# Decode attention with an MLP beside it: wq and wo read like keys inside the loop, and w1 added up by POOL

## The chip, the cores and the metric

The kernel runs on one core of a Trainium2 chip, all in float32. The metric is the time of one execution on the device in microseconds (us), as the median of several runs. Besides, the hardware profiler recorded one execution.

## The reference, cut to what matters

```python
xn = layernorm(x)                               # x: 512 numbers
q = (xn @ wq).reshape(32, 128)                  # wq: 512 x 4096; 32 heads of queries
k, v = repeat each of the 8 heads 4 times       # caches: 8 x 65536 x 128
p = softmax(q k^T / sqrt(128))
a = (p v).reshape(4096) @ wo                    # wo: 4096 x 512
b = relu(xn @ w1) @ w2                          # w1: 512 x 1792, w2: 1792 x 512
return x + a + b
```

There is one token. K and V are 268 MB each, wq and wo 8.4 MB each, w1 and w2 3.7 MB each: 561 MB that are read once.

## The kernel before, in words

K and V are taken as 32 chunks of 16384 positions, four chunks to each of the 8 key heads. One chunk is 8.4 MB. There is one buffer for K (`kt`), one for V (`vt`) and one for w1 and later w2 (`wt`), so a chunk's transfer can start only when the chunk before it in the same buffer has been used up.

All large transfers are issued by SP, one after the other, in the order of lines 135 to 156: wq in two halves into `vt`, w1 into `wt`, the first K into `kt`; then in a loop V after semaphore `vfree`, the next K after `kfree`; at the end wo in four parts into `kt`, and w2 in four parts into `wt`. SP waits at each of these semaphores, and what stands behind a wait in its list waits too. ACT issues two small transfers of x (L190, L192); in the first, each of the 128 partitions gets four numbers.

The head (before the loops). ACT, PE, DVE and POOL make the layer norm; POOL ends it with xn (L178 to L182). Element `p*4+a` of a vector lies on partition p, column a. DVE then multiplies the first two of wq's four blocks by xn and adds them (L338, L339), PE adds up the partitions and the other two blocks (L235) into one row, and DVE transposes that row into `qbig`. The same is done with w1 (L245), giving h, and `hT` after the ReLU (L356).

The loop over chunks on PE (L251): scores (L259), 8 rounds of four matmuls of 512 columns. The four go to four strips of 32 rows, c = 0 to 3, and run side by side; each pair of rounds fills two PSUM banks, which DVE transposes into `tr` (L365) and gives back by `free`. After the last pair DVE signals `kfree` (L364). DVE takes the maximum (L369 to L376), with the help of two small PE steps (L266, L268); ACT computes the exponentials (L212); PE multiplies them with V (L275, "PV"); DVE signals `vfree` (L378) and copies the result (L379), PE folds it (L282, L285), and DVE keeps the running sums (L381 to L384). In a float32 matmul PE records two weight loads and two matmuls, so 32 matmuls are 64 records.

The tail. When the last head's output `oT` is ready (L387), PE multiplies the last columns of oT with wo (L299), then hT with the first ten rows of blocks of w2 (L307), all added up in four strips of PSUM, `y4`. DVE adds x and copies y4 (L391); PE adds up the strips (L323) between the last four blocks of w2 (L316), which go to `yacc`. DVE copies (L393), and SP writes the output in four pieces of 512 bytes (L156). Then POOL waits for the output.

```python
take(sp, sem("vfree"))
sp.dma_start(vt, v_row[bass.ds(n, 1)]...).then_inc(sem("v"), 16)
take(sp, sem("kfree"))
sp.dma_start(kt, k[0, bass.ds(n + 1, 1)]...).then_inc(sem("k"), 16)
```

`take` is an instruction that waits for a semaphore and lowers it; it is recorded under line 48, and waits at it appear as "PEq L48" or "DVEq L48".

Of the kernel before, what the change touches and what calls it, by code (L numbers as in the profile page):

```python
# [8 lines left out]
AF = mybir.ActivationFunctionType  # L9
ALU = mybir.AluOpType  # L10
# [13 lines left out]

HKV = 1
# [6 lines left out]
TW = 512  # L32
SUB = TW // 32
CHUNK = 16384
NCH = SK // CHUNK
TPC = CHUNK // (CT * TW)
NB = CHUNK // P
XA = D // P
BANKS = 4
WIDE = 4  # L40
WO_CUTS = [8, 8, 8, 8]
# [4 lines left out]
def take(e, sem, n=1):  # L46

    return e.sem_inc(sem, -n).wait_op(sem, n, "sem-ge")  # L48


@with_exitstack
def attention_and_mlp_kernel(
# [25 lines left out]

    kt = sbuf("kt", P, CHUNK)
# [5 lines left out]
    qbig = sbuf("qbig", P, NQ, 32)  # L85
    hbig = sbuf("hbig", P, FB, 32)
    o_sb = sbuf("o_sb", P, WIDE, DH)
    ysum = sbuf("ysum", P, 512)
    x4 = sbuf("x4", P, 512)
# [11 lines left out]
    qpad = sbuf("qpad", P, 32)  # L101
    hT = sbuf("hT", P, FB)
    oT = sbuf("oT", P, NQ)
    m = sbuf("m", P, GROUP)
# [5 lines left out]
    corr = sbuf("corr", P, GROUP)  # L110
    part_sum = sbuf("part_sum", P, GROUP)
    l_run = sbuf("l_run", P, GROUP)
    o_run = sbuf("o_run", P, GROUP)
    ysb = sbuf("ysb", P, P)
# [3 lines left out]
    hrow = banks[:, 1024:1536]  # L118
    acc = banks[:, 2048:2560]
    pma = banks[:, 2560:3072]  # L120
    pmb = banks[:, 3072:3584]
    y4 = banks[:, 3584:]
    yacc = banks[:, :P]
# [6 lines left out]
    half = CHUNK // 2  # L130
    wo_at = [sum(WO_CUTS[:i]) for i in range(len(WO_CUTS) + 1)]
    w2_at = [sum(W2_CUTS[:i]) for i in range(len(W2_CUTS) + 1)]


    for i in range(2):
        cut = slice(i * half, (i + 1) * half)
        sp.dma_start(vt[:, cut], wq_row[:, cut]).then_inc(sem(f"wq{i}"), 16)
    sp.dma_start(wt, w1_row).then_inc(sem("w1"), 16)
    sp.dma_start(kt, k[0, 0]).then_inc(sem("k"), 16)
# [8 lines left out]
    for i in range(len(WO_CUTS)):  # L148
        cut = slice(wo_at[i] * D, wo_at[i + 1] * D)
        sp.dma_start(kt[:, cut], wo_row[:, cut]).then_inc(sem(f"wo{i}"), 16)  # L150
    sp.wait_ge(sem("wfree"), 1)
# [4 lines left out]
    sp.dma_start(out.rearrange("(c n) -> c n", c=CT), ysb[0:P:32, :]).then_inc(sem("out"), 16)  # L156


    def after(ins):

        ins.then_inc(sem("pool"), 1)
        take(pool, sem("pool"))

    pool.memset(x4, 0.0).then_inc(sem("x4z"), 1)
# [3 lines left out]
    after(pool.memset(ident, 0.0))  # L168
    after(pool.affine_select(
# [4 lines left out]
    after(pool.tensor_add(sel, places[0], places[1]))  # L174
    after(pool.tensor_add(sel, sel, places[2]))
    pool.tensor_add(sel, sel, places[3])
    pool.wait_ge(sem("ln"), 4)
    after(pool.tensor_mul(st[:, 6:7], st[:, 5:6], st[:, 5:6]))  # L178
    after(pool.tensor_mul(st[:, 6:7], st[:, 6:7], st[:, 3:4]))
    after(pool.tensor_scalar(st[:, 6:7], st[:, 6:7], -0.5, 1.5, op0=ALU.mult, op1=ALU.add))  # L180
    after(pool.tensor_mul(st[:, 7:8], st[:, 5:6], st[:, 6:7]))
    pool.tensor_scalar_mul(xn, xc, st[:, 7:8]).then_inc(sem("xn"), 1)  # L182
    pool.memset(qpad, 0.0)
    pool.memset(nb_run, 3.0e38)
    pool.memset(l_run, 0.0)
    pool.memset(o_run, 0.0).then_inc(sem("sel"), 1)
# [4 lines left out]
    act.wait_ge(sem("x4z"), 1)  # L191
    act.dma_start(x4[0:1, :], x.rearrange("(o n) -> o n", o=1)).then_inc(sem("x4"), 16)  # L192
# [15 lines left out]
    with act.Fori(0, NCH):  # L208
        take(act, sem("bias"))
        act.activation(corr, diff, AF.Exp)  # L210
# [8 lines left out]
    pe.wait_ge(sem("means"), 1)  # L219
    pe.wait_ge(sem("zero"), 1)  # L220
    pe.wait_ge(sem("ln"), 1)
    pe.matmul(pma[:, 0:1], minus, st[:, 0:1], start=True, stop=True).then_inc(sem("mean"), 1)
    pe.wait_ge(sem("ln"), 2)
    pe.matmul(pmb[:, 0:1], plus, st[:, 2:3], start=True, stop=True).then_inc(sem("mean"), 1)
    pe.wait_ge(sem("xn"), 1)
    for a in range(1, XA):
        if a == 1:
            pe.wait_ge(sem("sum"), 1)
        if a == 2:
            pe.wait_ge(sem("wq1"), 16)  # L230
        src, col = (tr2, ones[:, :1]) if a == 1 else (vt[:, a * NQ * DH : (a + 1) * NQ * DH], xn[:, a : a + 1])
        for i in range(2):
            heads = src.rearrange("p (i h e) -> p i h e", i=2, e=DH)[:, i]
            for c in range(CT):
                last = pe.matmul(  # L235
                    banks[32 * c : 32 * c + 1, i * 512 : (i + 1) * 512], col,
                    heads[:, :, 32 * c : 32 * c + 32], start=(a == 1), stop=(a == XA - 1),
                )
    last.then_inc(sem("qrow"), 1)
    pe.wait_ge(sem("sum"), 2)  # L240
    for a in range(1, XA):
        src, col = (tr2[:, :DFF_ALL], ones[:, :1]) if a == 1 else (wt[:, a * DFF_ALL : (a + 1) * DFF_ALL], xn[:, a : a + 1])
        blocks = src.rearrange("p (b e) -> p b e", e=P)
        for c in range(CT):
            last = pe.matmul(  # L245
                hrow[32 * c : 32 * c + 1, : FB * 32], col,
                blocks[:, :, 32 * c : 32 * c + 32], start=(a == 1), stop=(a == XA - 1),
            )
    last.then_inc(sem("hrow"), 1)
    pe.wait_ge(sem("sel"), 1)  # L250
    with pe.Fori(0, NCH):  # L251
        take(pe, sem("q"))
        take(pe, sem("k"), 16)
        for s in range(TPC):
            if s % 2 == 0:
                take(pe, sem("free"))
            for c in range(CT):
                lo = (s * CT + c) * TW
                last = pe.matmul(  # L259
                    pair[s // 2 % 2][32 * c : 32 * c + 32, s % 2 * 512 : s % 2 * 512 + 512], qpad,  # L260
                    kt[:, lo : lo + TW], start=True, stop=True,
                )
            if s % 2:
                last.then_inc(sem("score"), 1)
        take(pe, sem("m"))
        pe.transpose(pma[:GROUP, :P], m, ident).then_inc(sem("mT"), 1)  # L266
        take(pe, sem("dg"))
        pe.matmul(pmb[:, :GROUP], ones[:GROUP, :], dg, start=True, stop=True).then_inc(sem("nb"), 1)  # L268
        take(pe, sem("probs"))
        take(pe, sem("v"), 16)  # L270
        n = NB // WIDE
        for i in range(n):
            c = 32 * (i % CT)
            b = i * WIDE
            last = pe.matmul(  # L275
                acc[c : c + WIDE * GROUP, :],
                probs[:, b : b + WIDE, :].rearrange("p b g -> p (b g)"),
                vt[:, b * DH : (b + WIDE) * DH],
                start=(i < CT), stop=(i >= n - CT),
            )  # L280
        last.then_inc(sem("acc"), 1)
        pe.matmul(pma[:, 256 : 256 + GROUP], ones, part_sum, start=True, stop=True)  # L282
        take(pe, sem("o"))
        for b in range(WIDE):
            last = pe.matmul(  # L285
                pma[:, 264 : 264 + GROUP], o_sb[:, b, :], sel[:, b, :],
                start=(b == 0), stop=(b == WIDE - 1),
            )
        last.then_inc(sem("part"), 1)

    for j in range(NQ):
        if j in wo_at:
            pe.wait_ge(sem(f"wo{wo_at.index(j)}"), 16)
        if j == 0:
            pe.wait_ge(sem("oT"), HEADS - 1)
        if j == NQ - GROUP:
            pe.wait_ge(sem("oT"), HEADS)
        c = 32 * (j % CT)
        pe.matmul(  # L299
            y4[c : c + 1, :], oT[:, j : j + 1], kt[:, j * D : (j + 1) * D],  # L300
            start=(j < CT), stop=False,
        )
    for b in range(W2_ROWS):
        if b in w2_at:
            pe.wait_ge(sem(f"w2{w2_at.index(b)}"), 16)
        c = 32 * (b % CT)
        last = pe.matmul(  # L307
            y4[c : c + 1, :], hT[:, b : b + 1], wt[:, b * D : (b + 1) * D],
            start=False, stop=(b >= W2_ROWS - CT),
        )  # L310
    last.then_inc(sem("y4"), 1)
    for b in range(W2_ROWS, FB):
# [7 lines left out]
        if b + 1 == w2_at[-2]:  # L320
            pe.wait_ge(sem("ysum"), 1)
            for c in range(CT):
                pe.matmul(  # L323
                    yacc[32 * c : 32 * c + 1, :], sel[:, 0, :1], ysum[:, c * P : (c + 1) * P],
                    start=False, stop=False,
                )
    last.then_inc(sem("yacc"), 1)


    def then(ins):  # L330

        ins.then_inc(sem("dve"), 1)
        take(dve, sem("dve"))

    def add_first_two(src, n, name):

        dve.wait_ge(sem(name), 16)
        then(dve.tensor_scalar_mul(tr2[:, :n], src[:, :n], xn[:, 0:1]))  # L338
        dve.scalar_tensor_tensor(  # L339
# [83 lines left out]
```

## Time and profile before

| | us |
|---|---|
| median of 3 runs (1305.24 to 1305.49) | 1305.4 |
| the profiled execution | 1305.23 |
| its span, from first to last instruction | 1303.5 |
| PE busy | 685.0 |
| DVE busy | 282.3 |
| ACT busy | 75.4 |
| POOL busy | 3.4 |

In the rows of a timeline the first number is the start in us from the begin of the span, the second the time it took; then engine, line, operation, what it writes and reads, how many records were merged, and in brackets the idle time before it with what ended it. In the windows view the columns are: stretch, its length, busy time (and number of instructions) of PE, PEld, DVE, ACT and POOL, granted clock of PE, share of the 16 DMA engines that is busy, GB/s. DMA rows end with the us from issue to landing. Packets are counted in a window by their start or end, so that in short windows the share can go over 1.

### The profile page before, as it was taken

The page shows a single profiled execution, that of the slowest core. Times are in us where ns is not written, and L with a number is a line of the kernel's source. Part 1 is how long each engine was busy: PE and PEld are TensorE (multiplying, and loading weights), DVE is VectorE, ACT ScalarE, POOL GpSimd, SP SyncE. Part 2 cuts the span into 40 slices and gives each one's busy share as a digit, 9 for nine tenths or more (in the row PEclk, how much of TensorE's full clock was granted, in tenths as well). Part 3 has the DMA queues.
Part 4 walks back from the last instruction along what each step waited for, and adds up shares of the span by engine and source line. Part 5 has one row for each costly group of instructions (what it writes and reads, how often), then busy time and mean ns, then how long its engine had stood idle before and what let it go on. Part 6 is the DMA issues. An engine that isn't in the chain of part 4 may idle for free. (4 is left out here: it accounts for less than half of the span.)

```text
span 1303.5 us, 11851 instructions
## 1 busy us (share of the span) xinstructions
PE 685.0 (53%) x4712; PEld 210.0 (16%) x4712; DVE 282.3 (22%) x524; ACT 75.4 (6%) x299; POOL 3.4 (0%) x22
## 2 busy tenths in 40 slices
PE   1554654554554554564465465465456456456547
PEld 0111111111111111111111111111111111111111
DVE  3301222211222211222221122221122221122220
ACT  1000000000000000000000000000000000000000
POOL 1000000000000000000000000000000000000000
PEclk9767777867776776776677776777676776677678
DMA  9999999999999999999999999999999999999998
GB/s 402 451 419 448 420 448 418 451 417 448 420 438 430 426 442 422 446 422 446 422 446 422 446 418 451 418 448 420 440 428 430 438 422 446 422 446 422 446 415 345
DMA packets 10957, 561.04 MB, mean 430 GB/s; under 512 B 1349, under 2 KB 1353, under 8 KB 1610
## 3 DMA queue, kind: packets, MB, share of 16 engines
q1 hardware_dynamic: 10808, 561.00, 99.5%
q8 instruction: 2, 0.03, 0.0%
q10 hardware_dynamic: 146, 0.00, 0.0%
q14 instruction: 1, 0.01, 0.0%
HBM read 560.99 MB, written 0.00 MB: 430 GB/s over the span
## 5 line engine op out<-in xcount | busy, mean ns | idle before, releaser
L259 PE MATMUL banks<-kt,qpad 128*32 128x512 f32 x2048 | 297.7, 743 | 263.2 <-PEq L48 263.2
L275 PE MATMUL banks<-vt,probs 128*16 128x512 f32 x2048 | 293.5, 737 | 173.9 <-PEq L48 173.9
L365 DVE STREAM_TRANSPOSE tr<-banks 128x1024 f32<-128x1024 f32 x128 | 160.0, 1250 | 415.2 <-DVEq L48 415.2
L259 PEld LDWEIGHTS banks<-kt,qpad 128*32 128x32 f32 x2048 | 79.3, 132 | 456.8 <-issue 456.7
L275 PEld LDWEIGHTS banks<-vt,probs 128*16 128x16 f32 x2048 | 69.4, 113 | 371.3 <-issue 371.3
L379 DVE COPY o_sb<-banks 128x512 f32<-128x512 f32 x32 | 22.1, 691 | 446.0 <-DVEq L48 446.0
L210 ACT ACTIVATE corr<-diff 128x4 f32<-128x4 f32 x32 | 6.6, 205 | 1179.7 <-ACTq L48 1179.7
L212 ACT ACTIVATE probs<-tr,nb_new 128x128 f32<-128x128 f32 x128 | 63.8, 507 | 0.0
L266 PE MATMUL banks<-ident,m 128*4 128x128 f32 x32 | 10.1, 317 | 88.3 <-PEq L48 88.3
L285 PE MATMUL banks<-sel,o_sb 128*128 128x4 f32 x256 | 32.8, 252 | 25.4 <-PEq L48 25.4
L285 PEld LDWEIGHTS banks<-sel,o_sb 128*128 128x128 f32 x256 | 31.0, 191 | 27.2 <-issue 27.2
L369 DVE TENSOR_REDUCE m<-tr 128x4 f32<-128x512 f32 x32 | 32.2, 1006 | 2.9
L268 PE MATMUL banks<-dg,ones 4*128 4x4 f32 x64 | 14.3, 291 | 30.1 <-PEq L48 30.1
L212 ACT ACTIVATION_READ_ACCUMULATOR probs<-tr,nb_new 128x1 f32 x128 | 23.9, 187 | 0.0
L266 PEld LDWEIGHTS banks<-ident,m 128*4 128x4 f32 x32 | 2.6, 81 | 116.4 <-issue 116.4
L268 PEld LDWEIGHTS banks<-dg,ones 4*128 4x128 f32 x64 | 12.4, 240 | 37.7 <-issue 37.7
L381 DVE TENSOR_TENSOR l_run<-l_run,corr 128x4 f32<-128x4 f32 x32 | 5.2, 163 | 42.3 <-DVEq L48 42.3
L282 PEld LDWEIGHTS banks<-part_sum,ones 128*128 128x128 f32 x64 | 9.5, 188 | 27.2 <-issue 27.2
L371 DVE TENSOR_REDUCE mg<-banks 4x1 f32<-4x128 f32 x32 | 8.9, 279 | 19.6 <-DVEq L48 19.6
L282 PE MATMUL banks<-part_sum,ones 128*128 128x4 f32 x64 | 12.3, 263 | 0.0
L374 DVE TENSOR_TENSOR nb_new<-banks,nb_run 128x4 f32<-128x4 f32 x32 | 5.2, 162 | 23.8 <-DVEq L48 23.8
L235 PE MATMUL banks<-tr,ones 128*1 128x512 f32 x16 | 3.6, 1048 | 11.3 <-DVE tr L339 11.3
(74 smaller groups left out, 92.8 us busy)
## 6 DMA issues: line engine op xcount, KB each, us to landing
vt<-wq SPq DMA_DIRECT2D x2, 4096.0 KB, 16.8
kt<-wo SPq DMA_DIRECT2D x4, 2048.0 KB, 21.1
wt<-w SPq DMA_DIRECT2D x1, 3584.0 KB, 29.5
wt<-w SPq DMA_DIRECT2D x1, 1536.0 KB, 30.9
wt<-w SPq DMA_DIRECT2D x1, 1024.0 KB, 32.9
wt<-w SPq DMA_DIRECT2D x2, 512.0 KB, 34.1
kt<-k SPq DMA_DIRECT2D x32, 28.6
vt<-v SPq DMA_DIRECT2D x32, 29.2
```

The costliest lines, as they stand in the source:

```text
L210: act.activation(corr, diff, AF.Exp)
L212: last = act.activation(probs[:, :, g], tr[:, :, g], AF.Exp, bias=nb_new[:, g : g + 1], scale=scale, accum_out=part_sum[:, g : g + 1],)
L259: last = pe.matmul(pair[s // 2 % 2][32 * c : 32 * c + 32, s % 2 * 512 : s % 2 * 512 + 512], qpad, kt[:, lo : lo + TW], start=True, stop=True,)
L266: pe.transpose(pma[:GROUP, :P], m, ident).then_inc(sem("mT"), 1)
L268: pe.matmul(pmb[:, :GROUP], ones[:GROUP, :], dg, start=True, stop=True).then_inc(sem("nb"), 1)
L275: last = pe.matmul(acc[c : c + WIDE * GROUP, :], probs[:, b : b + WIDE, :].rearrange("p b g -> p (b g)"), vt[:, b * DH : (b + WIDE) * DH], ...
L282: pe.matmul(pma[:, 256 : 256 + GROUP], ones, part_sum, start=True, stop=True)
L285: last = pe.matmul(pma[:, 264 : 264 + GROUP], o_sb[:, b, :], sel[:, b, :], start=(b == 0), stop=(b == WIDE - 1),)
L365: dve.transpose(tr[:, s * 2 * SUB : (s + 1) * 2 * SUB, :].rearrange("p b i -> p (b i)"), pair[s % 2]).then_inc(sem("free"), 1)
L369: dve.reduce_max(m, tr.rearrange("p b i -> p i b")[:, :GROUP, :], axis=AX.X).then_inc(sem("m"), 1)
L371: then(dve.reduce_max(mg, pma[:GROUP, :P], axis=AX.X))
L379: dve.tensor_copy(o_sb.rearrange("p b d -> p (b d)"), acc).then_inc(sem("o"), 1)
```

## The change

Part by part:

- wq is loaded into `kt` (in three parts, 8192, 4096 and 4096 columns) and scored by PE like a chunk of keys, with xn in the first four columns of the query `qpad`. POOL copies xn there. DVE picks the needed products out of `tr` and adds them up into `qall` with one reduction. SP waits for `kfree` before the first K is issued.
- wo is loaded into `kt` in three parts at the end and scored in the same way with oT as the query; DVE reduces the result to `yT`, spreads it over a diagonal (`yd`), and one matmul of ones adds it into y4.
- The PE loop therefore has 34 turns. Each turn does, if it is not one of the first two, the four matmuls on the added-up w1 (with `kfree`), then the maximum, PV and the folding of the chunk before; and then the scores of the next chunk. In the first two turns the upper part is jumped over.
- POOL multiplies the four blocks of w1 by xn and adds them up in place: four products and three sums of 128x1792. h is read from PSUM only after the loop; hT comes from POOL, and w2 is issued after it.
- Around the loop stands another of two turns, and its body is under an If that is true only in the second turn. In the first turn PE jumps from the start of its code over the loop and comes back.
- K is laid out in memory so that a matmul of strip c reads 16 runs of 32 columns, 128 apart. The transfers have the same shapes as before.
- x goes into y4 as the row `xrow` by a matmul; the output leaves from 128 partitions, four numbers each. `vfree` and `kfree` come from PE; waits are put onto the instructions themselves in many places; running sums l and o are kept in one tile.

```diff
-TW = 512
-SUB = TW // 32
+TPC = 128
+SUB = 1
...
+ROUNDS = 8
+WQ_CUTS = [8192, 4096, 4096]
+WO_CUTS = [16, 8, 8]
...
+    hrow = pmb[:, 64:512]
...
+    def of_own_row(cols, groups):
+
+        return bass.AP(tr.tensor, tr.offset, [list(tr.ap[0]), [32, cols], [32 * cols + 1, groups]])
...
-        sp.dma_start(vt[:, cut], wq_row[:, cut]).then_inc(sem(f"wq{i}"), 16)
+    for i in range(len(WQ_CUTS)):
+        cut = slice(wq_at[i], wq_at[i + 1])
+        sp.dma_start(kt[:, cut], wq_row[:, cut]).then_inc(sem(f"wq{i}" if i else "k"), 16)
     sp.dma_start(wt, w1_row).then_inc(sem("w1"), 16)
+    take(sp, sem("kfree"))
     sp.dma_start(kt, k[0, 0]).then_inc(sem("k"), 16)
...
-    sp.wait_ge(sem("wfree"), 1)
+    sp.wait_ge(sem("hT"), 1)
...
+    sp.dma_start(out.rearrange("(p a) -> p a", p=P), ysb[:, 0, :]).then_inc(sem("out"), 16)
...
+    pool.memset(qpad, 0.0).then_inc(sem("vfree"), 1)
...
+    after(pool.tensor_copy(qpad[:, :XA], xn), "pool", chain[0]).then_inc(sem("q"), 1)
...
+    pool.wait_ge(sem("w1"), 16)
+    for a in range(XA):
+        last = pool.tensor_scalar_mul(w1_of[a], w1_of[a], xn[:, a : a + 1])
...
+    after(pool.tensor_add(w1_of[0], w1_of[0], w1_of[1]), "pool", chain[0])
+    link(pool.tensor_add(w1_of[2], w1_of[2], w1_of[3]))
+    after(pool.tensor_add(w1_of[0], w1_of[0], w1_of[2]), "pool", chain[0]).then_inc(sem("sum"), 1)
...
+    after(pool.tensor_scalar_max(hT, hbig[:, :, 0], 0.0), "hx").then_inc(sem("hT"), 1)
...
+    def tensor_loop():
...
+        with pe.Fori(0, NCH + 2) as t:
+            with pe.If(t > 1):
+                pe.wait_ge(sem("sum"), 1)
+                for c in range(CT):
+                    last = pe.matmul(
+                        hrow[32 * c : 32 * c + 1, :], ones[:, :1], hb[:, :, 32 * c : 32 * c + 32],
+                        start=True, stop=True,
+                    )
+                last.then_inc(sem("kfree"), 1)
...
+                pe.matmul(lo_new[:, 0, :], ones, part_sum, start=True, stop=True).then_inc(sem("vfree"), 1)
...
+            take(pe, sem("q"))
+            take(pe, sem("k"), 16)
+            for s in range(ROUNDS):
+                if s % 2 == 0:
+                    take(pe, sem("free"))
+                for c in range(CT):
+                    last = pe.matmul(
+                        pair[s // 2 % 2][32 * c : 32 * c + 32, s % 2 * 512 : s % 2 * 512 + 512], qpad,
+                        kb[:, s * 16 : s * 16 + 16, c, :], start=True, stop=True,
+                    )
...
+    with pe.Fori(0, 2) as turn:
+        with pe.If(turn > 0):
+            tensor_loop()
+
+    pe.wait_ge(sem("hT"), 1)
+    pe.wait_ge(sem("xrow"), 16)
+    pe.matmul(y4[0:1, :], ones[0:1, 0:1], xrow, start=True, stop=False)
...
+    after(
+        pe.matmul(y4[0:1, :], ones[:, :1], yd.rearrange("p q n -> p (q n)"), start=False, stop=True), "yd"
+    ).then_inc(sem("p2d"), 1)
...
+    def turn_scores(gates=(), free=None):
+
+        for s in range(ROUNDS // 2):
+            if free and s == ROUNDS // 2 - 1:
+                after(dve.nop(), "p2d", s + 1).then_inc(sem(free), 1)
+            ins = after(dve.transpose(tr2[:, s * 1024 : (s + 1) * 1024], pair[s % 2]), "p2d", s + 1)
+            if s < len(gates):
+                ins = after(dve.drain(), gates[s], 16)
+            ins.then_inc(sem("free"), 1)
...
+    turn_scores(["wq1", "wq2"], free="kfree")
+    dve.drain()
+    dve.tensor_reduce(qall, of_own_row(NQ, XA), axis=AX.X, op=ALU.add).then_inc(sem("dve"), 1)
...
+    dve.tensor_copy(qpad, oT).then_inc(sem("q"), 1)
+    dve.transpose(ysum[:, : FB * 32], hrow).then_inc(sem("hx"), 1)
+    turn_scores(["wo1", "wo2"])
+    dve.drain()
+    dve.tensor_reduce(yT, of_own_row(CT, NQ), axis=AX.X, op=ALU.add).then_inc(sem("dve"), 1)
+    after(
+        dve.tensor_mul(
+            yd, ident.unsqueeze(1).to_broadcast([P, CT, P]), yT.unsqueeze(2).to_broadcast([P, CT, P])
+        ), "dve",
+    ).then_inc(sem("yd"), 1)
+    after(dve.tensor_copy(ysum, y4), "p2d", 5).then_inc(sem("ysum"), 1)
```

More of the change, by code (lines that the diff above doesn't have):

```diff
@@ L48, in take, with starts @@
     return e.sem_inc(sem, -n).wait_op(sem, n, "sem-ge")
+def starts(cuts):
+    return [sum(cuts[:i]) for i in range(len(cuts) + 1)]
 @with_exitstack
@@ L129, in attention_and_mlp_kernel @@
     v_row = v[0].rearrange("(n p b) d -> n p (b d)", p=P, b=NB)
[L130 to L137, printed above, removed]
+    wq_at, wo_at, w2_at = starts(WQ_CUTS), starts(WO_CUTS), starts(W2_CUTS)
+    def of_own_row(cols, groups):
[3 more added lines that the diff above has]
+        sp.dma_start(kt[:, cut], wq_row[:, cut]).then_inc(sem(f"wq{i}" if i else "k"), 16)
     sp.dma_start(wt, w1_row).then_inc(sem("w1"), 16)
+    take(sp, sem("kfree"))
     sp.dma_start(kt, k[0, 0]).then_inc(sem("k"), 16)
@@ L155, in attention_and_mlp_kernel, with link @@
     sp.wait_ge(sem("y"), 1)
[L156 to L164, printed above, removed]
+    sp.dma_start(out.rearrange("(p a) -> p a", p=P), ysb[:, 0, :]).then_inc(sem("out"), 16)
+    chain = [0]
+    def link(ins):
+        if chain[0]:
+            after(ins, "pool", chain[0])
+        chain[0] += 1
+        return ins.then_inc(sem("pool"), 1)
     pool.memset(minus, -1.0 / D)
@@ L167, in attention_and_mlp_kernel @@
     pool.memset(eps, EPS).then_inc(sem("means"), 1)
[L168 to L169 removed]
+    link(pool.memset(ident, 0.0))
+    link(pool.affine_select(
         out=ident, in_=ident, compare_op=ALU.not_equal, fill=1.0, base=0,
@@ L181, in attention_and_mlp_kernel @@
[L181 to L186, printed above, removed]
+    link(pool.tensor_add(sel, places[0], places[1]))
+    link(pool.tensor_add(sel, sel, places[2]))
+    link(pool.tensor_add(sel, sel, places[3]))
+    pool.memset(qpad, 0.0).then_inc(sem("vfree"), 1)
+    pool.memset(nb_run, 3.0e38).then_inc(sem("free"), 2)
@@ new lines, in attention_and_mlp_kernel @@
+    w1_of = [wt[:, a * f : (a + 1) * f] for a in range(XA)]
+    pool.wait_ge(sem("w1"), 16)
+    for a in range(XA):
+        last = pool.tensor_scalar_mul(w1_of[a], w1_of[a], xn[:, a : a + 1])
+    last.then_inc(sem("pool"), 1)
+    chain[0] += 1
+    after(pool.tensor_add(w1_of[0], w1_of[0], w1_of[1]), "pool", chain[0])
+    link(pool.tensor_add(w1_of[2], w1_of[2], w1_of[3]))
+    after(pool.tensor_add(w1_of[0], w1_of[0], w1_of[2]), "pool", chain[0]).then_inc(sem("sum"), 1)
+    hbig = ysum[:, : FB * 32].rearrange("p (b i) -> p b i", i=32)
@@ L216, in attention_and_mlp_kernel @@
         last.then_inc(sem("probs"), 1)
[L219 to L302, printed above, removed]
+    kb = kt.rearrange("p (b c e) -> p b c e", c=CT, e=32)
+    hb = wt[:, :f].rearrange("p (b e) -> p b e", e=P)
@@ L323, in attention_and_mlp_kernel @@
                 pe.matmul(
-                    yacc[32 * c : 32 * c + 1, :], sel[:, 0, :1], ysum[:, c * P : (c + 1) * P],
+                    yacc[32 * c : 32 * c + 1, :], ones[:, :1], ysum[:, c * P : (c + 1) * P],
                     start=False, stop=False,
                 )
[L327 to L339, printed above, removed]
-            tr2[:, :n], src[:, n : 2 * n], xn[:, 1:2], tr2[:, :n], op0=ALU.mult, op1=ALU.add
-        ).then_inc(sem("sum"), 1)
+    last.then_inc(sem("p2d"), 1)
```

152 lines of the change are left out of this document (82 added, 70 removed).

## The prediction, made before the changed kernel was run

> **What bounds the kernel now.** I read the page first, for the queues and for the chain that ended last.
>
> ```profile
> q1 hardware_dynamic: 10808, 561.00, 99.5%
> q8 instruction: 2, 0.03, 0.0%
> ...
> DMA wt<-w 3%; SPq L150 0%; SPq L154 0%; PE banks L316 0%; DVE ysb L393 0%
> ```
>
> One queue, SP's, keeps the 16 DMA engines busy for 99.5% of the span, and the chain ends in the last weight transfer. No compute engine sets the pace. How far compute is from setting it shows the timeline of PE, DVE and SP in the first iterations.
>
> ```profile
> 50.99 9.18 PE L259 MATMUL banks<-kt,qpad 128*32 128x512 f32 x64 [6.96 <-PEq L48]
> 60.43 1.25 DVE L365 STREAM_TRANSPOSE tr<-banks 128x1024 f32<-128x1024 f32 x1 [0.62 <-DVEq L48]
> 60.58 0.34 SPq L144 DMA_DIRECT2D kt<-k  x1
> 70.16 9.75 PE L275 MATMUL banks<-vt,probs 128*16 128x512 f32 x64 [5.67 <-PEq L48]
> 91.07 9.61 PE L259 MATMUL banks<-kt,qpad 128*32 128x512 f32 x64 [9.03 <-PEq L48]
> 110.28 8.47 PE L275 MATMUL banks<-vt,probs 128*16 128x512 f32 x64 [4.97 <-PEq L48]
> 129.78 9.04 PE L259 MATMUL banks<-kt,qpad 128*32 128x512 f32 x64 [8.89 <-PEq L48]
> ```
>
> PE starts on a chunk when it has landed. The next K is issued at 60.58 while V lands only near 70.1, so the queue never runs dry: 9.5 us to spare. From 91.07 to 129.78 lie two chunks, 19.35 us each. But from V at 70.16 to K at 91.07 it is 20.91 us, where the same step later takes 129.78 - 110.28 = 19.50. So 1.41 us were lost once. In that stretch lies one of the two packets of q8, 16 KB of instructions; the other lies between 270 and 300 us. The DMA view of the two stretches:
>
> ```profile
> q8 instruction: 1, 0.02, 0.3%
> q8 instruction: 1, 0.02, 0.2%
> ```
>
> My reading: a packet puts one DMA engine behind, and since each transfer is split evenly over the engines, every landing after it waits for that engine. A second packet on another engine then costs nothing more. The end agrees; the view by windows, whose last but one column is the DMA share:
>
> ```profile
> 1297.00:1297.50 0.50, 0.47 (x8) 0.10 (x8) 0.00 (x0) 0.00 (x0) 0.00 (x0) 1.00 0.69 270
> 1297.50:1298.00 0.50, 0.50 (x8) 0.00 (x0) 0.00 (x0) 0.00 (x0) 0.00 (x0) 1.00 0.19 74
> 1298.50:1299.00 0.50, 0.44 (x20) 0.14 (x12) 0.40 (x1) 0.00 (x0) 0.00 (x0) 1.00 0.12 49
> ```
>
> A share of 0.19 is three engines of 16, 0.12 two: they run alone for up to 1.3 us. So the time before is even streaming, about 1.3 us of stragglers, and a head and a tail of some microseconds. Only these can change by much.
>
> **The change part by part.**
>
> *The main loop.* The same bytes land in the same order. K is now laid out so that a matmul reads 16 runs of 32 columns. The old wq code read such runs:
>
> ```profile
> 13.73 0.56 PE L222 MATMUL banks<-st,minus 128*128 128x1 f32 x2 [13.73 <-ACT xc L199]
> 19.90 0.30 POOL L182 TENSOR_SCALAR xn<-xc,st 128x4 f32<-128x4 f32 x1 [0.21 <-POOLq L48]
> 30.74 3.87 PE L235 MATMUL banks<-vt,xn 128*1 128x512 f32 x32
> ```
>
> That is 0.48 us per four records, against 9.18 / 16 = 0.57 for K, so nothing is lost. K's release now comes from PE, after its back edge, the If and one group of four w1 matmuls. With 1 to 2 us for the group by the same rows and some for branches I take 2, allow 4, and 9.5 are to spare: nothing. Were that cover gone, each microsecond would cost one per chunk. V's release moves from DVE to PE at about the same moment, and DVE's fewer small operations are as hidden as before.
>
> *The head.* Before, wq lay in vt, so K's first chunk was queued at once behind w1. Now wq lies in kt, and SP waits for the wq scores before it issues K; the first V and everything else stand behind K in SP's order.
>
> ```profile
> 0.91 0.87 SPq L137 DMA_DIRECT2D vt<-wq  x2
> 1.82 0.45 SPq L138 DMA_DIRECT2D wt<-w  x1
> 2.31 0.67 SPq L139 DMA_DIRECT2D kt<-k  x1
> ```
> ```profile
> wt<-w SPq DMA_DIRECT2D x1, 3584.0 KB, 29.5
> xT<-x ACTq DMA_DIRECT2D x1, 2.0 KB, 12.4
> kt<-k SPq DMA_DIRECT2D x1, 48.4
> ```
> ```profile
> 1.80:2.00 0.20, 0.00 (x0) 0.00 (x0) 0.00 (x0) 0.00 (x0) 0.16 (x2) 1.00 2.39 655
> ```
>
> xn is ready at 20.20; its copy to qpad takes another 0.3; the wq scores are a full key chunk, 9.2 us (I bound them by 8.4 and 10.1, since the half-speed clock that follows an idle stretch ends at varying moments: 9.18, 9.61 and 9.04 above); the release and SP take 0.4 (60.58 against 50.99 + 9.18). The later parts of wq have landed by then. K is issued at 30.1. In an idle queue the first bytes move 0.9 us after the issue (0.91 to 1.8), and I allow the last engine 0.9 more. Before, K's landing was seen at 2.31 + 48.4 = 50.7. Issued at 30.1 it is seen at 30.1 + 0.9 to 1.8 + 19.35 + some 0.4 until a landing is seen: 50.8 to 51.7. So the **gap** is 0.1 to 1.0 us; with the bounds of the scoring, from hidden to 1.9. I take 0.8, near the upper end, because the slowest engine decides.
>
> *The stragglers.* PE has less code outside its loop (the 36 matmuls of wq and w1 and the 32 of wo are gone), and it touches its second page in the first microseconds, while it has nothing to do until 13.73. If the q8 packets are its own, they leave the stretch in which they cost something: an engine 1.4 us behind near 30 us catches up in the gap. At the end 1.3 us can go, at least nothing (if packets come all the same); one of the three may stay. I take -0.8.
>
> *POOL* now adds up w1 in seven operations of 128x1792, from w1's landing at 1.82 + 29.5 = 31.3 on. No row has such an operation on POOL.
>
> ```profile
> L338 DVE TENSOR_SCALAR tr<-wt,xn 128x1792 f32<-128x1792 f32 x1 | 1.1, 1112 | 0.0
> L339 DVE SCALAR_TENSOR_TENSOR tr<-wt,xn,tr 128x1792 f32<-128x1792 f32 x1 | 2.1, 2085 | 0.1
> L175 POOL TENSOR_TENSOR sel<-sel,ident 128x16 f32<-128x16 f32 x1 | 0.2, 220 | 0.2 <-POOLq L48 0.2
> L178 POOL TENSOR_TENSOR st<-st 128x1 f32<-128x1 f32 x1 | 0.2, 193 | 14.6 <-DVE st L346 14.6
> L180 POOL TENSOR_SCALAR st<-st 128x1 f32<-128x1 f32 x1 | 0.2, 190 | 0.2 <-POOLq L48 0.2
> ```
>
> DVE's rows for the size give 4 x 1.11 + 3 x 2.09 = 10.7 us, the lower bound. POOL's TENSOR_TENSOR grows by 27 ns for 15 elements, 1.8 ns each, so 3.4 us an operation and 24 in all. The upper bound is TENSOR_SCALAR, 190 to 299 ns for three elements more: 65 us an operation. I take 24, since that row differs by elements alone. PE needs the sum for K's release, and all of PE's loop stands behind that wait. The next K must be issued by about 68, so the sum is due at 66: 35 us for 24, nothing. [...]
>
> *The tail.* wo was 16 groups of matmuls whose first 24 hid behind its landing; now it is a full scoring.
>
> ```profile
> 1284.89 0.17 DVE L387 TENSOR_TENSOR oT<-o_run,diff 128x4 f32 x1
> 1290.84 1.90 PE L299 MATMUL banks<-kt,oT 128*1 128x512 f32 x16 [0.50 <-DMA kt<-wo]
> 1297.03 1.04 PE L307 MATMUL banks<-wt,hT 128*1 128x512 f32 x8 [0.61 <-DMA wt<-w]
> 1298.21 0.69 DVE L391 TENSOR_TENSOR ysum<-banks,x 128x512 f32<-128x512 f32 x1 [13.16 <-PE banks L307]
> 1298.96 0.40 PE L323 MATMUL banks<-ysum,sel 128*1 128x128 f32 x8
> 1299.48 0.62 PE L316 MATMUL banks<-wt,hT 128*1 128x128 f32 x16
> 1300.16 0.29 DVE L393 COPY ysb<-banks 128x128 f32<-128x128 f32 x1 [1.26 <-PE banks L316]
> 1300.48 0.66 SPq L156 DMA_DIRECT2D y<-ysb  x1
> ```
>
> oT is ready at 1285.06 and qpad by 1285.4; with 9.3 us scoring ends at 1294.7. A group of four strips is 0.86 us (1.90 for two, 1.04 for one: 0.18 is latency). On strip 0 follow the x row, b=0 and b=4, to 1297.3, then w2's second part, to 1298.2, and the new yd matmul, to 1299.1; before, y4 was complete at 1298.07. DVE's copy (0.14 + 0.69), ysum's matmuls (0.46), the last two rows (0.68) and the transpose (0.35) lead to 1301.4, against 1300.48 before: **+0.95**, from +0.75 (scoring of 8.4, w2 sets the start) to +1.65 (10.1). yd hides: DVE's last transpose ends at 1296.3, and a reduction and a product of 512 elements, under 1.4 together by the 0.69 of L391, end before 1298.2; later than that, each microsecond costs one. w2 is now issued after hT, and only the output stands behind that wait: 1285.4, a transpose under 1.25, a short POOL step, so 1287.0, first bytes 1287.9 to 1288.8. wo streams to 1290.8, on early engines to 1289.4: hidden by a little. The output goes out in 128 pieces instead of 4. The nearest row is x, 128 pieces, 12.4 us, but each of an engine's 8 pieces waits there for a wq packet of 32 KB, 1.2 us at 433 GB/s / 16. Without these 9.7 us, 2.7 remain, no more than the 3.0 from 1300.48 to the end of the 1303.5 us span. I take 0 and allow 0.8.
>
> Sum against the profiled execution: 1305.23 + 0.8 - 0.8 + 0.95 = 1306.2. The median of before lies 0.17 above its profiled execution, so **1306.4**.
>
> **The rivals.** About 0.2%, 2.6 us, is what a measurement of this kernel can tell from no change.
>
> (B) The change doesn't do what it says: instruction packets still come while the stream is full. Then 0.8 isn't gained: 1307.2, by the bounds up to 1308.5. For it: the second packet came in mid-loop, where no new code begins. Chance 0.18.
>
> (C) A little faster: scoring of 8.4 hides the gap and all stragglers go, 0 - 1.3 + 0.75: 1304.9. Chance 0.14.
>
> (D) Slower, by pages fetched again. If the If and the back edge drop a page at each pass, two packets come per pass, 66 in all. Each puts one engine 1.4 us behind; spread evenly over 16 that is 5.8 us, and the 0.8 isn't gained: 1313. It decides from about 30 packets on. Against it: 32 back edges before brought two packets. [...] Chance 0.07.
>
> (E) POOL needs more than 35 us: at 7 us an operation the sum ends at 80 and one K is 13 us late: 1319. Chance 0.03.
>
> (F) Head and tail both long: slow clock in both scorings, or PE back from its second page after 13.73. Gap 1.9, stragglers -0.4, tail and output 2.4: 1309.3. Chance 0.10.
>
> **How the numbers follow.** The forecast has 0.48; its own bounds are those of its three terms. The range from 1304.6 to 1309.4 takes in B, C and F and leaves out D, E and some edges. Faster by over 0.2% would be below 1302.8, for which neither head nor tail has room: 0.02, C's edge. Slower: D, E, F and 0.03 of B, 0.23. Within: 0.75.
>
> **What would show it.** In the profile after: PE's first scores near 20.6, for 9 us; the first K issued near 30, and a dip of the DMA share of under a microsecond behind w1; q8 packets, if any, before 30; no step of 20.9 us between chunks; fewer stragglers in the last windows; and 2 us instead of 1.05 between the last landing and the output's issue. A first K issued well after 31, a K released later than V lands, or tens of q8 packets would make the prediction wrong.

## The result, and the profile after

The changed kernel takes **1307.4 us** (median of 22 runs, 1305.7 to 1309.4), the one before 1305.3 (22 runs beside it, 1305.1 to 1306.6). The ratio is 1.0015, with a 95% interval of 1.001 to 1.0021. The change costs 2.1 us: little, but the interval leaves out no change. Its profiled execution took 1308.47 us, with a span of 1306.8, so it lies 1.1 above the median; the times read from it below are to be taken with that reserve.

The page of the changed kernel:

```profile
q1 hardware_dynamic: 10944, 561.00, 99.3%
q8 instruction: 1, 0.02, 0.0%
...
DMA wt<-w 1%; PE banks L315 0%; PE banks L320 0%; DVE ysum L392 0%; DVE ysum L383 0%; PE banks L326 0%; DVE ysb L394 0%; PE banks L333 0%; SPq L167 0%; POOL hT L214 0%; DVE qpad L382 0%; DVEq L358 0%
...
xT<-x ACTq DMA_DIRECT2D x1, 2.0 KB, 13.8
```

SP's queue still fills the DMA engines, now for 99.3% instead of 99.5%; 0.2% of 1306.8 us are 2.6 us. There is one q8 packet where there were two; the DMA view from 4 to 8 us has it:

```profile
q8 instruction: 1, 0.02, 1.4%
```

By its start it comes at 5.3 us. x comes 1.4 us later than before (13.8 for 12.4). The timeline of its head and first chunks:

```profile
14.70 0.20 ACT L227 ACTIVATE xc<-xT 128x4 f32<-128x4 f32 x1 [11.51 <-DMA xT<-x]
...
21.94 9.10 PE L297 MATMUL banks<-kt,qpad 128*32 128x512 f32 x64 [4.46 <-PEq L49]
...
31.23 0.33 SPq L152 DMA_DIRECT2D kt<-k  x1
...
32.88 19.12 POOL L207 TENSOR_SCALAR wt<-wt,xn 128x1792 f32<-128x1792 f32 x4 [11.38 <-DMA wt<-w]
...
33.27 4.43 DVE L359 COPY qpad<-qall 128x4 f32 x1 [0.34 <-DVEq L49]
...
52.09 3.96 POOL L210 TENSOR_TENSOR wt<-wt 128x1792 f32<-128x1792 f32 x1
...
55.33 9.47 PE L297 MATMUL banks<-kt,qpad 128*32 128x512 f32 x64 [24.29 <-PEq L49]
...
64.19 0.11 PEld L261 LDWEIGHTS banks<-wt,ones 128*1 128x1 f32 x4 [0.30 <-POOL wt L212]
...
65.82 0.34 SPq L157 DMA_DIRECT2D kt<-k  x1
...
74.54 8.39 PE L276 MATMUL banks<-vt,probs 128*16 128x512 f32 x64 [5.85 <-PEq L49]
...
94.04 8.89 PE L297 MATMUL banks<-kt,qpad 128*32 128x512 f32 x64 [9.18 <-PEq L49]
```

POOL starts when it has seen w1 land (32.88), and PE's second scoring when it has seen K land (55.33): 22.45 us, where K alone needs 19.35. From there the pace is that of before: 19.50 from V to the next K, and no step of 20.9. K's second chunk is issued at 65.82, over 8 us before V is seen at 74.54. Its tail:

```profile
1286.34 0.16 DVE L379 TENSOR_TENSOR oT<-lo_run,diff 128x4 f32 x1
...
1287.43 5.36 PE L297 MATMUL banks<-kt,qpad 128*32 128x512 f32 x48 [1.92 <-PEq L49]
...
1287.91 1.75 SPq L167 DMA_DIRECT2D wt<-w  x4
...
1299.97 1.04 PE L315 MATMUL banks<-wt,hT 128*1 128x512 f32 x8 [0.62 <-DMA wt<-w]
...
1302.87 0.62 PE L326 MATMUL banks<-wt,hT 128*1 128x128 f32 x16
...
1303.99 0.34 SPq L169 DMA_DIRECT2D y<-ysb  x1
```

And the windows of its last transfers:

```profile
1299.50:1300.00 0.50, 0.03 (x4) 0.03 (x8) 0.00 (x0) 0.00 (x0) 0.00 (x0) 1.00 0.31 123
1300.00:1300.50 0.50, 0.50 (x8) 0.16 (x9) 0.00 (x0) 0.00 (x0) 0.00 (x0) 1.00 0.06 25
1300.50:1301.00 0.50, 0.50 (x9) 0.08 (x2) 0.00 (x0) 0.00 (x0) 0.00 (x0) 1.00 0.08 33
```

A share of 0.06 is a single engine of 16, still moving weights when the others are done. So a straggler is there at the end: one where before had three, and later than any of those.

A landing is seen when the slowest engine is done. Each large transfer ends with 16 packets of 4 bytes, as many as there are DMA engines: before, those of w1 came from 30.40 to 30.91 us, and w1 was seen at 31.3; in the changed kernel 15 came by 30.86 and one at 32.47, and POOL started at 32.88. So I worked out from the packets of each trace (their starts and durations) when each engine had ended a transfer; and as a packet in the full stream begins within 0.01 us of the end of the one before it on its engine, also which engine carried a q8 packet. The table has the median engine's end, in us from the begin of the span, and behind it how much later the slowest was. The last column is the time from the slowest engine's end of w2 to the issue of the output:

```
                               w1            first K        last part of w2   to the output
before                     30.67 +0.24      50.00 +0.25      1297.40 +1.59        1.49
after                      30.56 +1.90      52.39 +2.33      1299.65 +2.27        2.06
no early visit             30.72 +0.17      51.25 +0.36      1298.58 +1.37        2.54
first K in halves          30.67 +1.83      50.50 +1.66      1297.71 +1.70        2.00
yd early                   30.66 +1.81      52.31 +2.59      1299.88 +2.42        1.61
small first wq piece       30.76 +1.40      50.11 +1.40      1297.52 +1.28        2.09
small piece, yd early      30.70 +1.84      50.25 +1.63      1297.50 +1.69        1.60
the same, no early visit   30.70 +0.37      50.03 +0.38      1297.46 +1.50        1.60
before, with a visit       30.76 +3.00      50.08 +3.04      1297.67 +2.81        2.49
three sums more on POOL    30.63 +1.81      53.20 +0.19      1308.67 +0.23        2.72
```

From w1 to the first K the median engine of the changed kernel takes 21.83 us, 2.5 over the transfer's 19.35: that is the gap. Between the two profiled executions the span's 3.4 us (1306.85 less 1303.45) come apart as follows: the slowest engine ends w2 2.93 later (1301.93 for 1298.99), of which the median engine has 2.25 and the straggler 0.68; from there to the output's issue it takes 0.57 more (the same, 4.02 instead of 3.45, if counted from w2's second part seen); from the output's issue to the span's end 2.86 instead of 2.97.

### The profile page after: what moved, and what is told of

Same layout as the page of the kernel before. It is cut to its first block, busy times and chain, and to the rows that moved or that the text cites. A ratio compares the mean times of both kernels' runs of the same rounds, so it can differ in the third digit from the quotient of the medians.

```text
span 1306.8 us, 11976 instructions
## 1 busy us (share of the span) xinstructions
PE 704.1 (54%) x4964; PEld 217.0 (17%) x4964; DVE 279.1 (21%) x466; ACT 75.4 (6%) x299; POOL 34.4 (3%) x29
## 3 DMA queue, kind: packets, MB, share of 16 engines
q1 hardware_dynamic: 10944, 561.00, 99.3%
## 5 line engine op out<-in xcount | busy, mean ns | idle before, releaser
L297 PE MATMUL banks<-kt,qpad 128*32 128x512 f32 x2176 | 314.4, 742 | 289.9 <-PEq L49 289.9
L345 DVE STREAM_TRANSPOSE tr<-banks 128x1024 f32<-128x1024 f32 x136 | 170.0, 1250 | 449.0 <-PE banks L297 447.5
L297 PEld LDWEIGHTS banks<-kt,qpad 128*32 128x32 f32 x2176 | 85.1, 133 | 492.1 <-issue 492.0
L238 ACT ACTIVATE corr<-diff 128x8 f32<-128x8 f32 x32 | 6.7, 208 | 1179.8 <-ACTq L49 1179.8
L261 PE MATMUL banks<-wt,ones 128*1 128x448 f32 x256 | 30.1, 539 | 0.0
L269 PE MATMUL banks<-dg,ones 4*128 4x4 f32 x64 | 11.2, 244 | 22.9 <-PEq L49 22.9
L207 POOL TENSOR_SCALAR wt<-wt,xn 128x1792 f32<-128x1792 f32 x4 | 19.1, 4797 | 11.4 <-DMA wt<-w 11.4
L269 PEld LDWEIGHTS banks<-dg,ones 4*128 4x128 f32 x64 | 9.4, 183 | 28.9 <-issue 28.9
L374 DVE TENSOR_TENSOR lo_run<-lo_run,banks 128x8 f32<-128x8 f32 x32 | 5.2, 163 | 40.0 <-DVEq L49 40.0
```

Of the source, the lines that this page charges most:

```text
L207: last = pool.tensor_scalar_mul(w1_of[a], w1_of[a], xn[:, a : a + 1])
L261: last = pe.matmul(hrow[32 * c : 32 * c + 1, :], ones[:, :1], hb[:, :, 32 * c : 32 * c + 32], start=True, stop=True,)
L297: last = pe.matmul(pair[s // 2 % 2][32 * c : 32 * c + 32, s % 2 * 512 : s % 2 * 512 + 512], qpad, kb[:, s * 16 : s * 16 + 16, c, :], start ...
L345: ins = after(dve.transpose(tr2[:, s * 1024 : (s + 1) * 1024], pair[s % 2]), "p2d", s + 1)
```

## The experiments

Each ratio is to the kernel before, run on the same chip. The theory that I formed from the two traces: the head costs the time, by K's late issue, and the visit (PE's early jump over its loop and back) only moves a fetch, the q8 packet, which now falls into wq's transfer. Against it stands the prediction's own account (the visit saves the stragglers, and the tail costs 1 us), and for each part the rival named with it.

**The early visit taken out.**

```diff
-    with pe.Fori(0, 2) as turn:
-        with pe.If(turn > 0):
-            tensor_loop()
+    tensor_loop()
```

> Only the outer loop of two turns is taken away, so PE walks straight into its loop. Theory A (the time over before is lost in the head: the fetched page puts one DMA engine behind, so x lands at 14.7 instead of 13.3 and the first K is issued later into an empty queue): x lands near 13.3 again, xn is ready 1.2 earlier, the first K is issued near 30, and the time is 1306.0 to 1306.8. Rival (the visit to the second page pays, since PE would otherwise stop for that page at its first jump to the scores): PE's first scores begin 2 us or more after q is ready, the first K is issued after 31.2, and the time is 1308 to 1310.

1307.24 us (1306.01 to 1308.37), 1.0013 [1.0004, 1.0022]: no different from the changed kernel. Its timeline:

```profile
13.23 0.20 ACT L227 ACTIVATE xc<-xT 128x4 f32<-128x4 f32 x1 [10.04 <-DMA xT<-x]
...
20.49 9.44 PE L297 MATMUL banks<-kt,qpad 128*32 128x512 f32 x64 [4.48 <-PEq L49]
...
30.12 0.33 SPq L152 DMA_DIRECT2D kt<-k  x1
...
52.25 8.92 PE L297 MATMUL banks<-kt,qpad 128*32 128x512 f32 x64 [22.32 <-PEq L49]
...
90.92 8.37 PE L297 MATMUL banks<-kt,qpad 128*32 128x512 f32 x64 [8.02 <-PEq L49]
...
111.33 8.38 PE L276 MATMUL banks<-vt,probs 128*16 128x512 f32 x64 [8.15 <-PEq L49]
...
1286.08 9.82 PE L297 MATMUL banks<-kt,qpad 128*32 128x512 f32 x64 [1.95 <-PEq L49]
...
1296.77 2.74 PE L313 MATMUL banks<-wt,hT 128*1 128x512 f32 x20
```

And its DMA view from 90 to 110 us:

```profile
q8 instruction: 1, 0.02, 0.3%
```

Without the visit x is there at 13.23, as before the change, K is issued at 30.12, where the prediction had it, and no engine is behind at w1 or at K. But the packet then comes at about 102 us, and with it the step of 20.4 us (90.92 to 111.33) and an engine 1.4 us behind at the end. So the visit moves the fetch and doesn't remove what it costs: it puts an engine behind at 5 us instead of at 102.

Part of what the head gains without the visit is lost in the tail. In the profiled executions the stream ends 1.97 us earlier than in the changed kernel (1299.95 for 1301.93), but the output is issued only 1.5 earlier. Here wo's scores took 9.82 us, at a granted clock of 0.72 (1.00 in the changed kernel), and PE came to the rows of w2 behind them, with no wait for a landing left.

**The first K in two halves**, the first issued after two of the four rounds of wq scores.

```diff
-    sp.dma_start(kt, k[0, 0]).then_inc(sem("k"), 16)
+    sp.dma_start(kt[:, :half], k[0, 0][:, :half]).then_inc(sem("k"), 16)
+    take(sp, sem("kfree"))
+    sp.dma_start(kt[:, half:], k[0, 0][:, half:]).then_inc(sem("kh"), 16)
...
-            if free and s == ROUNDS // 2 - 1:
+            if free and s % 2:
...
+    dve.wait_ge(sem("kh"), 16)
```

DVE's copy of the first head's query now waits for the second half.

> The first K comes in two halves, the first released when the first half of the wq scores is done (near 27). Theory A: the DMA queue no longer runs dry behind w1, the 2.4 us gap of the head goes, every later landing is some 2.2 earlier, and the time is 1305.0 to 1305.8. Rival (the loss is in the main loop, where K is released later by PE, or in the tail): the gap goes but the time stays at 1307 or above.

1306.5 us (1305.93 to 1307.74), 1.0009 [1.0, 1.0018]. Its timeline:

```profile
27.59 0.33 SPq L153 DMA_DIRECT2D kt<-k  x1
...
31.11 0.33 SPq L155 DMA_DIRECT2D kt<-k  x1
...
52.76 3.49 DVE L363 COPY qpad<-qall 128x4 f32 x1 [19.94 <-DMA kt<-k]
```

With the first half issued 3.6 us earlier than in the changed kernel, the gap shrinks from 2.5 to 0.5 us (30.67 to 50.50 is 19.83), and the median of the times by 0.9, though the two intervals overlap. That speaks for the gap as a part of the cost.

**The yd product between the first and the second part of w2**, so that it isn't behind the second.

```diff
+        if b + 1 == w2_at[1]:
+            after(
+                pe.matmul(y4[0:1, :], ones[:, :1], yd.rearrange("p q n -> p (q n)"), start=False, stop=False), "yd"
+            )
...
```

> The yd matmul is put between the first and the second part of the w2 rows. Theory A (the chain y4, copy, ysum sets the tail, and yd lies in it with 0.85): the output is issued 0.4 to 0.9 sooner after the last landing, time 1306.5 to 1307.0. Rival (the last landing sets the tail, as a straggling engine is late): no change, 1307.4.

1307.77 us (1305.83 to 1308.89), 1.0017 [1.0008, 1.0026]: no gain. Its timeline:

```profile
1299.54 1.02 PE L321 MATMUL banks<-yd,ones 128*1 128x512 f32 x2
...
1302.78 0.62 PE L328 MATMUL banks<-wt,hT 128*1 128x128 f32 x16 [0.16 <-DMA wt<-w]
...
1303.90 0.34 SPq L169 DMA_DIRECT2D y<-ysb  x1
```

yd is out of the way, and from the slowest engine's end to the output's issue it takes 1.61 us instead of 2.06, as theory A had it. But the last matmuls now wait for w2's last part, on the engine that is 2.4 us behind, and that engine ended 0.37 later than in the changed kernel (1302.30 for 1301.93), so that the output goes out within 0.1 us of the one there. In the changed kernel that landing hid below the longer chain of PE and DVE. Nothing shows that the later landing comes from the edit. The runs of this kernel spread over 3.1 us, so that a gain of half a microsecond isn't ruled out by the times.

**A small first piece of wq**, 1 MB instead of 4, so that x shares its DMA engines with 8 KB packets.

```diff
-WQ_CUTS = [8192, 4096, 4096]
+WQ_CUTS = [2048, 6144, 4096, 4096]
...
+    pool.wait_ge(sem("wqx"), 16)
```

The first piece has a semaphore of its own, for which POOL waits ahead of its copy of xn.

> The first 2048 columns of wq are a transfer of their own, so each of the 8 pieces of x on an engine waits for an 8 KB packet of wq instead of a 32 KB one. Theory A: x lands near 6 to 7 instead of 14.7, xn is ready by 13, the wq scores end by 25 (they wait for the last part of wq, near 22.3), the first K is issued before w1 has landed, no gap, time 1305.0 to 1305.8. Rival (x is late for another reason, or the page keeps PE away until about 13): x or PE's first small matmul stays after 12, and the time stays above 1306.8.

1305.63 us (1305.26 to 1307.43), 1.0002 [0.9992, 1.0011], before being 1305.39 there. Its timeline:

```profile
7.21 0.21 ACT L228 ACTIVATE xc<-xT 128x4 f32<-128x4 f32 x1 [4.02 <-DMA xT<-x]
...
14.62 7.04 PE L298 MATMUL banks<-kt,qpad 128*32 128x512 f32 x48 [4.63 <-PEq L49]
...
24.32 3.14 PE L298 MATMUL banks<-kt,qpad 128*32 128x512 f32 x16 [2.66 <-PEq L49]
...
27.63 0.33 SPq L152 DMA_DIRECT2D kt<-k  x1
...
32.72 19.12 POOL L208 TENSOR_SCALAR wt<-wt,xn 128x1792 f32<-128x1792 f32 x4 [18.71 <-DMA wt<-w]
...
52.27 8.71 PE L298 MATMUL banks<-kt,qpad 128*32 128x512 f32 x64 [24.81 <-PEq L49]
...
1300.88 0.34 SPq L169 DMA_DIRECT2D y<-ysb  x1
```

x lands 7.5 us earlier, the scores run behind the parts of wq, and K is issued while w1 still streams. From w1 seen to K seen it is 19.55 us instead of 22.45, and the gap of the median engine is 0.0. The visit and a straggler (1.4) are still there, and the tail is as long as in the changed kernel (2.09 and 2.06). This edit alone gives back about 1.8 of the 2.1 us: the head's gap is the largest part of the cost. It isn't all: in the profiled executions the median engine ends the stream 2.1 us earlier than in the changed kernel, and the straggler is 1.0 us smaller.

**The small piece with yd early.**

> The small first piece of wq (as in the kernel before this one in the list of experiments that had no gap, 1305.63) and the yd matmul ahead of the second part of the w2 rows. Theory A (with the gap gone, the last landing is no longer late, and the chain over yd sets the tail with 0.57 over before): the output is issued 0.3 to 0.6 sooner, 1305.1 to 1305.4. Rival (the straggling engine's last landing sets the tail here too): 1305.6, no change.

1305.63 us (1304.88 to 1307.16), 1.0002 [0.9993, 1.0011], equal to the small piece alone. From the slowest engine's end to the output's issue it takes 1.60 us instead of 2.09, but the last matmuls again wait for the last landing, which came 0.39 later here, and the output goes out within 0.1 us of the run above:

```profile
1299.67 0.62 PE L329 MATMUL banks<-wt,hT 128*1 128x128 f32 x16 [0.17 <-DMA wt<-w]
...
1300.79 0.34 SPq L169 DMA_DIRECT2D y<-ysb  x1
```

**The same without the visit.**

> The same without the outer loop of two turns. Theory A (the page fetch only changes its place; one engine is 1.4 behind wherever the fetch falls into a full stream): x lands about 1 us sooner, a q8 packet comes later in the stream, and the time is that of the kernel with the outer loop within 0.4. Rival (the visit pays): 1 us slower; rival (the visit costs): 1 us faster.

1305.4 us (1304.95 to 1307.35), 1.0001 [0.9991, 1.001]. x lands at 6.11 and K is issued at 25.30, but the q8 packet comes between 130 and 150 us and one engine is 1.5 us behind at the end. It has the lowest median of the variants, and it equals the kernel before; none that I ran beats it.

**The kernel before with such a visit:** PE's code up to the tail in an outer loop of two turns.

```diff
+    def tensor_loop():
...
+    with pe.Fori(0, 2) as turn:
+        with pe.If(turn > 0):
+            tensor_loop()
```

> The kernel before with only the outer loop of two turns around PE's code up to its tail. Theory A (an engine that is put behind in a stream without a gap stays behind, whenever it happens): a q8 packet comes near 5, no step of 20.9 us near 70 to 91, a straggler of about 1.4 us at the end all the same, time 1305.4 within 0.4. The prediction's step on stragglers (the early visit takes the fetch out of the stretch in which it costs): 1304.1 to 1304.7.

1306.82 us (1305.46 to 1307.99), 1.0006 [0.9997, 1.0015]. From the page and the timeline:

```profile
q8 instruction: 5, 0.08, 0.0%
```
```profile
16.16 0.20 ACT L199 ACTIVATE xc<-xT 128x4 f32<-128x4 f32 x1 [12.82 <-DMA xT<-x]
...
53.84 9.10 PE L260 MATMUL banks<-kt,qpad 128*32 128x512 f32 x64 [7.04 <-PEq L48]
```

I had both accounts wrong here. There are five packets instead of two, three of them before 12 us; three engines are 3.0, 2.6 and 1.1 us behind at w1, and x and the first K are seen 2.9 us later than before the edit. In its median the visit costs 1.4 us, though the interval doesn't exclude nothing. In the profiled execution, whose span is 2.5 us longer than before, 1.2 of them are the larger straggler, and 1.0 comes behind it: PE did the rows of w2 at a granted clock of 0.50 (1296 to 1300 us), where before it had 1.00. Which branch brought which of the five packets, and which code a packet holds, no view shows.

**Three sums more on POOL** ahead of its signal, of 128x1792 each; their result isn't used.

```diff
+    for i in range(3):
+        link(pool.tensor_add(w1_of[1], w1_of[1], w1_of[2]))
...
```

> The changed kernel with three more sums of 128x1792 on POOL ahead of its signal (their result is not used). Theory A (POOL's 31 us are hidden with only some 8 us to spare, since the next K must be issued before V lands near 74): the sum ends near 76 instead of 64, K is issued near 78, the queue runs dry once for 4 to 6 us, and the time is 1311 to 1313. Rival (the main loop has much more room, as the prediction's 35 us against 24 said): under 1309.

1315.63 us (1315.11 to 1317.09), 1.0075 [1.006, 1.0091], 8.2 over the changed kernel where I expected 4 to 6. Its timeline:

```profile
31.94 0.33 SPq L152 DMA_DIRECT2D kt<-k  x1
...
32.83 19.12 POOL L207 TENSOR_SCALAR wt<-wt,xn 128x1792 f32<-128x1792 f32 x4 [11.52 <-DMA wt<-w]
...
54.00 9.24 PE L300 MATMUL banks<-kt,qpad 128*32 128x512 f32 x64 [22.25 <-PEq L49]
...
64.13 12.03 POOL L214 TENSOR_TENSOR wt<-wt 128x1792 f32<-128x1792 f32 x3
...
76.26 1.67 PE L264 MATMUL banks<-wt,ones 128*1 128x448 f32 x8 [13.02 <-POOLq L215]
...
78.21 0.34 SPq L157 DMA_DIRECT2D kt<-k  x1
...
100.37 9.94 PE L300 MATMUL banks<-kt,qpad 128*32 128x512 f32 x64 [7.20 <-PEq L49]
```

The 12.03 us of sums push K's issue from 65.82 to 78.21, 12.4 later. V's last engine ended at 72.72 here, so the issue is 5.5 us late; by the packets the median engine ends K 26.9 us after V, 7.5 more than a transfer takes. The other 2.0 us are the restart of an idle queue. My expectation had the lateness too small: it took V's landing near 74 from the changed kernel, where one engine was 2.3 us behind.

## Why the prediction came out as it did

The time lies in the range, and within the 0.2% of no change to which I gave the most chance, 1.0 us above the forecast. Of its steps those of the main loop, the tail and the output held in kind, the gap was mis-sized, and that of the stragglers failed.

*The main loop, nothing:* held. The pace is 19.35 us, and K is issued over 8 us before V is seen, though PE's release now stands behind POOL and the first w1 matmuls.

*The gap, +0.8:* the mechanism is right, shown by the halves and the small piece, which bring it to 0.5 and 0.0 and the median of the times down by 0.9 and 1.8 us; the size was 2.5. The wq scores themselves took 9.10 us, within the bounds. These came from the half-speed clock: in the windows of before it is 0.50 from 46 to 51 and from 84 to 91 us, where PE waits, still 0.50 from 51 to 55 and from 91 to 96, and 1.00 from 55.3 and from 96.2 on, in scorings of 9.18 and 9.61 us. Two parts were too small. K was issued at 31.23 instead of 30.1, because x came at 14.70 and not at 13.29. Each engine's share of x waits there for packets of wq (32 KB, 1.21 us each), and the engine that carried the q8 packet at 5.3 us was late with everything after it: that packet took 0.92 us and the packet of wq behind it 1.71, and its last piece of x came at 14.02, where the others' had come by 12.65. Without the visit K was issued at 30.12. And the restart takes longer than my 0.9 to 1.8 us: even in the run without the visit, with K at 30.12, the gap is 1.2 (30.72 to 51.25 is 20.53). By the packets of that trace, the first 64 KB of K on an engine after the pause take 3.08 us in the median, and 2.42 in the stream; the prediction had nothing for that.

*The stragglers, -0.8:* failed, in the sentence that an engine 1.4 us behind near 30 us catches up in the gap. The packet did move to 5.3 us, but into a stream that is full already (SP's queue fills 95.6% from 4 to 8 us), so the engine was behind at once: 1.9 at w1, 2.3 at K, 2.3 at the end, where before had 1.6. By that it is rival B's condition that came in (packets come while the stream is full), and 1307.2 was its time, 0.2 below the one measured; but that is luck, since its gap was still 0.8. Why the gap didn't absorb it, the packets show in part: in the changed kernel the other engines begin K from 32.19 on, while the slow one is on w1 until 32.46, and its own first packet of K begins only 1.8 us after that. So it is with yd early (32.01 and 32.47, and 2.6 behind at K). In the run with three sums more, the same code up to there, K was issued 0.7 us later, the slow engine was done at 32.44 and all 16 began from 32.89 on: 0.19 behind, and K seen at 54.00, 1.3 us earlier than in the changed kernel. Three executions agree that a straggler is absorbed if it is done when the others restart; what holds its packet back otherwise stays open. This toss of some 2 us, with fractions of a us in the head to decide it, would also make the runs of the changed kernel spread over 3.7 us where those of before spread over 1.5; that wasn't tested by itself.

*The tail, +0.95:* measured +0.57, below my bound of +0.75. Its condition came in, w2's second part set the start (PE waits for it at 1299.97). w2 was issued at 1287.91, 0.9 us later than worked out, since oT came late, and was hidden, as forecast. The other end of the term came in as well: in the runs without the visit and with three sums more, wo's scores took 9.82 and 9.89 us at a granted clock of 0.72 and 0.71, and the stretch behind the slowest engine was 1.05 and 1.23 longer than before. With yd out of it (three experiments) that stretch is only some 0.1 longer than before, so yd makes most of the 0.57; but the medians of the times show no gain from it, and there the last matmuls wait for the last landing.

*The output, 0:* -0.1 from issue to end of span. *POOL, 24 us of 35:* it took 31.2 (32.88 to 64.09), hidden, since K was issued over 8 us before V was seen. The adds took 3.96 to 4.02 us, not 3.4, and the multiplications 4.8, 19.12 for four, not 3.4: the prediction had one price for both, and on POOL the multiplication by a scalar is the dearer of the two, the other way round from DVE's rows (1.11 and 2.09). Rival E's mechanism is real, and the run with three sums more gives its price: 5.5 us late became 7.5 in the stream and 8.2 in the time.

*Rival D*, a page fetched again at each pass, didn't come: one packet in the whole run.

In sum for the profiled execution: +2.48 for the gap, less 0.23 of smaller differences between the median engines, +0.68 for the straggler, +0.57 for the tail, -0.11 for the output make the 3.4 us of the span; the prediction had +0.8, -0.8, +0.95 and 0. Gap and stragglers were off by 1.7 and 1.5 us, in the same direction. That the forecast was off by only 1.0 is luck: the tail and the output were smaller, and the profiled execution, by which the terms are measured, was 1.1 above the median.

## What to carry to other kernels

Where one queue is the bound, look at the few places at which its issuer has to wait for compute, and follow that wait back to its first input: here a transfer of 2 KB behind large packets set the whole head, and a smaller first piece of the large transfer was worth more than all else that was tried (about 1.8 of the 2.1 us). Moving an instruction fetch was worth nothing here, where it landed in a stream as full as the one it left (1307.4 us with the visit, 1307.24 without). And before shortening a chain at the end, see which landing is next behind it.

## What the runs showed of the hardware that was not expected

- Where POOL worked on 128x1792 in SBUF, a DVE copy of 128x4 from SBUF took 4.43 us (33.27 in the changed kernel) and 3.49 (52.76 in the run with two halves) and ended within 0.05 us of POOL's instruction at that moment. With POOL idle the same copy takes 0.17 (29.67 in the run with the small piece). What held it beside POOL, no view shows. DVE's transposes out of PSUM were not slowed: in the changed kernel 1.25 us beside POOL (61.43) and without it (64.86). Here the copy was hidden.
- An engine that had carried a q8 packet in the full stream stayed behind to the end: without the visit it was 1.5 us behind in the first chunk after the packet (near 110 us) and 1.4 at the end, and 1.3 to 1.7 us at the end in the other runs with a small gap or none. The run with three sums more had K landing with 0.19 between the engines after its first pause, a second pause of some 7 us, and 0.23 at the end. Not every straggler is one of these: with the small piece a second engine was 1.2 us behind from the first K on, and the only packet of the span had come at 4.8 us; its cause stays open.
- The small transfer of x was paced by the packets of the large one beside it: it was there at 13.2 us beside packets of 32 KB, and at 6.1 beside those of 8 KB (both without the visit).
